# Regrouped score and value matmuls, two row transposes in every auction step, and six float64 weight units converted after the experts

## The chip, the cores and the metric

The kernel runs on one core of a Trainium2 chip. The metric is the device time of one execution in microseconds (us). TensorE multiplies, ScalarE (ACT), VectorE (DVE) and GpSimd (POOL) work beside it, and SyncE's queue (SP) issues nearly all transfers.

## What is computed

Attention with a sigmoid in place of the softmax, then a mixture of experts in which each expert takes exactly 224 tokens by a greedy auction, then a dense layer with a squared ReLU:

```python
attn = 1 / (1 + np.exp(-(q @ k.T / np.sqrt(64) - np.log(448))))   # 4 batches, 12 heads, 448 tokens
x = (attn @ v)                                                    # as 1792 rows of 768
logits = x @ w_gate                                               # 8 experts; greedy, 224 tokens each
h = np.maximum(x[mask] @ w1[e], 0) @ w2[e]                        # w1 768x1024, w2 1024x768
g = s * np.maximum(h @ w_in, 0) ** 2 + b                          # w_in 768x2048, float64
out = g @ w_out                                                   # w_out 2048x768, float64
```

`w_in` and `w_out` arrive as float64. The kernel reads them as pairs of 32-bit words and rebuilds float32 with integer operations.

## The kernel before

**Attention** goes over 24 pairs of heads (`pairs`, six to a batch). For pair n the scores are four chunks of 112 keys. A chunk is two matmuls, one for each head, that stand in different halves of the array's rows (64 rows each) and write one `psc` tile of two banks; ACT turns it into a chunk of `attn` by a sigmoid (L238). The values of pair i are eight matmuls into one bank `pv`, the two heads in different halves of the array's columns; ACT copies it to `xT` (L252 before). `scores_av(n, i)` writes both together: two score chunks of the next pair, two value chunks of this pair, two score chunks, two value chunks. `psc` has two buffers (`ps_s`), `pv` two, and the router's small tiles `plg` and `pt` one each (`ps_l`). `mid` puts the router's matmuls (`gate`, `gate_turn`) between the chunks: a part of them stands inside a pair of score chunks.

**The conversion** of the float64 weights runs on DVE below attention: 32 units of 768 KB come in (`cv_in`, `craw`, three buffers), four DVE instructions make float32 (`convert`, L155 to L158), and 384 KB go out to `narrow` in device memory (`cv_out`). `CONV` says how many units each pair converts. All loads and stores of this part are issued in program order by SP; at most eight of them are under way, since each of the eight DMA semaphores is waited for before it is used again. `load_qk` runs three pairs ahead, `load_v` two.

**The auction** follows: `gate_last` and `prefs` finish the logits, then ten steps (`auction`) each make one small matmul chain through DVE and ACT. While they run, PE turns `xT` back into rows: one turn is four transposes into `px` (three buffers), one ACT copy to `xrow` and one store to `xs`; the first four stores are issued by ACT (`SYNC`), the rest by SP. `ROWS` says how many turns each step makes; one turn stands ahead of the first step. After the last step, `places` builds the index lists, and `gather(0)` fetches the first expert's rows once all of `xs` is written.

**Four groups** of two experts follow. Each group ends with the dense layer for its 448 tokens: a second stage of 16 blocks `f` (18 matmuls each, then ReLU on ACT and three DVE instructions that write `gt`) and a third stage of two halves `h` over 8 weight units, whose sums go to the tile `orow` and are scattered to the output. `advance` keeps the weights ahead: it loads a unit (`raw`, four buffers), rounds it on ACT (`wh`, up to five units ahead of the use) and takes the remainder on DVE or POOL (`wl`, up to four ahead, that is three whole blocks before it is multiplied). Units come in the order of use; the 32 converted units are used in every group.

Of the kernel before, what the change touches and what calls it, by code (L numbers as in the profile page):

```python
# [40 lines left out]
ROWS = (2, 2, 2, 3, 3, 3, 2, 2, 2, 2)  # L41
SYNC = 4
SIGNS = 2
CONV = [1, 1, 2, 1, 2] * 4 + [1, 2, 1]
# [17 lines left out]
def tile_kernel(ctx, tc, qT, kT, v, wg, w1, w2, wi, wo, s2, b2, cst, out):  # L62
# [69 lines left out]
    todo, coming, cout, craw = list(range(len(wide))), [], [], {}  # L132
# [13 lines left out]

    def convert():
        if not coming:
            return
        i = coming.pop(0)  # L150
        r = craw.pop(i)
        lo, hi = r[:, :, 0], r[:, :, 1]
        b = cgp.tile([128, 768], I32, name="cb_", bufs=2)
        a = cgp.tile([128, 768], I32, name="co", bufs=3)
        V.tensor_scalar(a, hi, 3, 0x3FFFFFFF, op0=ALU.logical_shift_left, op1=ALU.bitwise_and)  # L155
        V.tensor_scalar(b, lo.bitcast(U32), 2.0 ** -29, None, op0=ALU.mult)
        V.scalar_tensor_tensor(a, hi, -(1 << 30), a, op0=ALU.bitwise_and, op1=ALU.bitwise_or)
        V.tensor_tensor(a, a, b, op=ALU.add)  # L158
        cout.append((i, a))
        cv_out(1)  # L160
        cv_in()
# [48 lines left out]
    def load_v(i):  # L210
        b, p = pairs[i]
        vt[i] = vp.tile([CP, NC, 128], F32, name="vt", bufs=4)
        nc.sync.dma_start(vt[i], v[b, p])
# [9 lines left out]
    def scores_av(n, i, mid):  # L223
        if n is not None:
            rq, rk = raw_qk.pop(n)
            attn[n] = at.tile([CP, 2, NC, S], F32, name="attn")
        if i is not None:
            a = attn.pop(i)
            pv = ps_v.tile([128, 512], F32, name="pv")
        for c2 in range(0, NC, 2):  # L230
            for c in (c2, c2 + 1):
                mid(c)
                if n is not None:
                    p = ps_s.tile([CP, 2, 512], F32, name="psc")
                    for j in range(2):
                        me = slice(j * D, (j + 1) * D)
                        T.matmul(p[:, j, :S], rk[me, c * CP:(c + 1) * CP], rq[me], start=True, stop=True)  # L237
                    A.activation(attn[n][:, :, c, :], p[:, :, :S], AF.Sigmoid, bias=nls[:CP],  # L238
                                 scale=1.0 / math.sqrt(D))
            for c in (c2, c2 + 1):  # L240
                if i is not None:
                    for j in range(2):
                        T.matmul(pv[j * 64:(j + 1) * 64, :S], vt[i][:, c, j * D:(j + 1) * D], a[:, j, c, :],  # L243
                                 start=(c == 0), stop=(c == NC - 1))
        if i is not None:
            b, p = pairs[i]
            xt = xT[:, p, b * S:(b + 1) * S]
            if i == len(pairs) - 1:
                A.copy(xt[:, :2 * CP], pv[:, :2 * CP])
                A.copy(xt[:, 2 * CP:], pv[:, 2 * CP:S])  # L250
            else:
                A.copy(xt, pv[:, :S])  # L252

    def gate(b, p0, p1, last):
        if p0 == 0:
            plg[b] = ps_l.tile([128, 512], F32, name="plg")
# [9 lines left out]
    def gate_turn(b, stop):  # L266
        lg = lgs.pop(b)
        pt = ps_l.tile([128, 512], F32, name="pt")
# [21 lines left out]
    def bracket(stage):  # L290
# [4 lines left out]
        elif stage == 1:  # L295
            pm = ps_l.tile([128, 512], F32, name="plg")
# [4 lines left out]
        else:  # L301
            pr = ps_l.tile([128, 512], F32, name="plg")
# [31 lines left out]
    cv_in()  # L334
    cv_in()
    cv_in()
    scores_av(0, None, lambda c: None)
# [14 lines left out]
    for i in range(N):  # L352
        b, p = pairs[i]
        if i + 2 < N:
            load_v(i + 2)
        if i + 3 < N:
            load_qk(i + 3)
        def mid(c):
            if b == B - 1 and p == 5:
                if c == 0:  # L360
                    gate(b, 0, 5, 5)
                elif c == 2:
                    gate_copy(b)
                elif c == 3:
                    gate_turn(b, False)
            elif p == 5 and c == 0:
                gate(b, 0, 4, 6)
            elif p == 0 and b and c == 1:
                gate(b - 1, 4, 6, 6)
            elif p == 0 and b and c == 3:  # L370
                gate_copy(b - 1)
            elif p == 1 and b and c == 0:
                gate_turn(b - 1, True)

        scores_av(i + 1 if i + 1 < N else None, i, mid)
        if p == 1 and b:
            prefs(b - 1)
        if b == B - 1 and 2 <= p <= 4:
            bracket(p - 2)
# [5 lines left out]
        if i < N - 1:  # L385
            for _ in range(CONV[i]):
                convert()
    gate_last(B - 1)
# [33 lines left out]
    got = rows_in(1)  # L422
# [288 lines left out]

    stores, out_rows = [], []
# [4 lines left out]
    for g in range(4):  # L717
# [7 lines left out]
        gn = gt[:, :, :, t0:t0 + S]  # L725
        for f in range(KG):
# [7 lines left out]
            V.tensor_scalar(gn[:, f, 0], r, sb2[:, 1:2], None, op0=ALU.add)  # L734
# [4 lines left out]
            advance()  # L739
        gather(2 * g + 3)  # L740
# [96 lines left out]
```

## Time and profile before

| | us |
|---|---|
| median of 3 runs | 968.11 (963.48 to 972.67) |
| the profiled execution | 965.9 |
| its span in the trace | 964.1 |
| PE busy | 937.4 (97% of the span) |
| PEld (weight loads, beside PE) | 782.4 (81%) |
| DVE busy | 563.9 (58%) |
| ACT busy | 443.8 (46%) |
| POOL busy | 137.4 (14%) |

PE's busy time counts each matmul with a modelled end, so 97% is not 97% of its peak. The granted clock of PE is 1.00 (2.4 GHz) in all of attention and nearly all of the groups, and 0.50 (1.2 GHz) in most of the auction. A row of a timeline is the start, the time, the engine, the line, the operation and its tiles, how many were merged, and in square brackets the idle time ahead of it and what ended it.

### The profile page before, as it was taken

The numbers are of one execution on the slowest core, as the hardware profiler recorded it, in microseconds if no ns is written. First come the engines' busy times: TensorE is split into PE (matmuls) and PEld (weight loads), VectorE is DVE, ScalarE is ACT, GpSimd is POOL, SyncE is SP. The second block draws the span as 40 slices with busy tenths as digits, with TensorE's granted clock in tenths as the row PEclk, the third lists the DMA queues.
The fourth block names the chain that finished last, engine by engine and source line by source line (L and its number), as shares of the span: only waits on it lengthen the run. The fifth ranks groups of instructions, "written<-read, shape, count | busy, mean of one in ns | idle before, by whom it ended". The sixth has DMA issues, their size and how long they took to land.

```text
span 964.1 us, 14094 instructions
## 1 busy us (share of the span) xinstructions
PE 937.4 (97%) x5277; PEld 782.4 (81%) x5277; DVE 563.9 (58%) x1015; ACT 443.8 (46%) x771; POOL 137.4 (14%) x136
## 2 busy tenths in 40 slices
PE   9999999778999999999999999999999999999997
PEld 3333333466899999999999999999999999999997
DVE  3565635764777774278677321877774278677320
ACT  5666666573564332266533223664332266433220
POOL 1000001223330000153100002430000152100001
PEclk9999999857999999999999999999999999999999
DMA  8999996272674434477443433774434476533411
GB/s 288 380 318 360 351 374 230 98 228 79 208 232 145 124 114 137 131 244 234 142 138 108 127 99 91 262 233 147 118 116 140 131 235 204 152 121 109 119 46 66
DMA packets 68456, 173.08 MB, mean 180 GB/s; under 512 B 7968, under 2 KB 24864, under 8 KB 68384
## 3 DMA queue, kind: packets, MB, share of 16 engines
q1 hardware_dynamic: 64256, 160.22, 51.5%
q0 software_dynamic: 2272, 11.01, 3.3%
q10 hardware_dynamic: 1856, 0.92, 0.3%
q8 instruction: 42, 0.69, 0.3%
q14 instruction: 30, 0.25, 0.1%
HBM read 148.52 MB, written 23.59 MB: 179 GB/s over the span
## 4 chain that ended last, share of the span: by engine, by line
PE 82%; DVE 6%; DMA 5%; issue 3%; ACT 2%; POOL 1%; SPq 1%; POOLq 0%; ACTq 0%; DVEq 0%
PE acc L642 9%; PE acc L708 8%; PE acc L710 8%; PE acc L709 8%; PE acc L759 8%; PE acc L761 8%; PE acc L760 8%; PE pv L243 7%; PE psc L237 7%; PE acc L643 5%; DVE wl L198 2%; DMA raw<-in_w_dram 2%; DMA rq<-in_qT_dram 2%; PE px L409 2%; ACT wh L187 1%
## 5 line engine op out<-in xcount | busy, mean ns | idle before, releaser
L187 ACT CAST wh<-raw 128x768 fp32r<-128x768 f32 (+1 forms) x240 | 209.2, 878 | 160.1 <-PE acc L761 133.8
L198 DVE TENSOR_TENSOR wl<-raw,wh 128x768 fp32r<-128x768 f32 (+1 forms) x198 | 210.5, 1068 | 104.9 <-ACT wh L187 104.9
L198 POOL TENSOR_TENSOR wl<-raw,wh 128x768 fp32r<-128x768 f32 (+1 forms) x42 | 92.1, 2201 | 433.4 <-ACT wh L187 285.2
L759 PE MATMUL acc<-wh,gt 128*128 128x384 f32 x448 | 149.9, 335 | 0.0
L760 PE MATMUL acc<-wl,gt 128*128 128x384 f32 x448 | 149.7, 334 | 0.0
L761 PE MATMUL acc<-wh,gt 128*128 128x384 f32 x448 | 149.6, 334 | 0.0
L708 PE MATMUL acc<-y,wh 128*128 128x448 f32 x384 | 141.4, 368 | 0.0
L710 PE MATMUL acc<-y,wl 128*128 128x448 f32 x384 | 140.6, 366 | 0.0
L709 PE MATMUL acc<-y,wh 128*128 128x448 f32 x384 | 140.6, 366 | 0.0
L642 PE MATMUL acc<-u,wh 128*128 128x448 f32 x384 | 121.7, 375 | 1.7 <-DVE u L666 1.5
L238 ACT ACTIVATE attn<-psc,nls 112x896 f32<-112x896 f32 x96 | 92.1, 1005 | 53.8 <-PE psc L237 53.8
L732 ACT ACTIVATE r<-acc 128x448 f32<-128x448 f32 x64 | 34.9, 545 | 150.9 <-PE acc L710 150.9
L643 PE MATMUL acc<-u,wl 128*128 128x224 f32 x384 | 101.5, 264 | 0.0
L642 PE MATMUL acc<-x,wh 128*128 128x448 f32 x288 | 95.3, 385 | 0.0
L237 PE MATMUL psc<-rq,rk 64*112 64x448 f32 x384 | 85.6, 561 | 1.1 <-ACT attn L238 0.6
L760 PEld LDWEIGHTS acc<-wl,gt 128*128 128x128 f32 x448 | 84.1, 188 | 0.0
L759 PEld LDWEIGHTS acc<-wh,gt 128*128 128x128 f32 x448 | 84.1, 188 | 0.0
L761 PEld LDWEIGHTS acc<-wh,gt 128*128 128x128 f32 x448 | 84.1, 188 | 0.0
L243 PE MATMUL pv<-attn,vt 112*64 112x448 f32 x384 | 82.8, 552 | 0.0
L643 PE MATMUL acc<-x,wl 128*128 128x224 f32 x288 | 77.2, 268 | 2.1 <-POOL wl L198 2.1
L733 DVE SCALAR_TENSOR_TENSOR r<-r,sb 128x448 f32<-128x448 f32 x64 | 43.8, 685 | 60.4 <-ACT r L732 60.3
L642 PEld LDWEIGHTS acc<-u,wh 128*128 128x128 f32 x384 | 72.0, 188 | 8.6 <-DVE u L666 3.3
(214 smaller groups left out, 1245.3 us busy)
## 6 DMA issues: line engine op xcount, KB each, us to landing
raw<-nw SPq DMA_DIRECT2D x128, 384.0 KB, 3.0
raw<-in_w_dram SPq DMA_DIRECT2D x64, 384.0 KB, 3.7
raw<-in_w_dram SPq DMA_DIRECT2D x48, 512.0 KB, 4.4
craw<-in_wi_dram SPq DMA_DIRECT2D x16, 768.0 KB, 7.6
nw<-co SPq DMA_DIRECT2D x32, 384.0 KB, 8.0
craw<-in_wo_dram SPq DMA_DIRECT2D x16, 768.0 KB, 6.9
rk<-in_kT_dram SPq DMA_DIRECT2D x24, 224.0 KB, 9.2
rq<-in_qT_dram SPq DMA_DIRECT2D x24, 224.0 KB, 8.4
```

The source lines that it names most:

```text
L187: A.copy(h[:, :k], raws[i][:, :k])
L198: eng.tensor_sub(lo[:, :k], r[:, :k], h[:, :k].bitcast(F32))
L237: T.matmul(p[:, j, :S], rk[me, c * CP:(c + 1) * CP], rq[me], start=True, stop=True)
L243: T.matmul(pv[j * 64:(j + 1) * 64, :S], vt[i][:, c, j * D:(j + 1) * D], a[:, j, c, :], start=(c == 0), stop=(c == NC - 1))
L642: T.matmul(p[:, :2 * CAP], wh[:, k], src[:, k].rearrange("p a s -> p (a s)"), start=(k == 0), stop=False)
L643: T.matmul(p[:, :CAP], wl[:, k], src[:, k, 0], start=False, stop=(k == n - 1))
L708: T.matmul(p, wh, src[:, k, 0], start=first, stop=False)
L709: T.matmul(p, wh, src[:, k, 1], start=False, stop=False)
L710: T.matmul(p, wl, src[:, k, 0], start=False, stop=last)
L759: T.matmul(ps[t][:, :DH], hi, wh[:, cols], start=(f == 0), stop=False)
L760: T.matmul(ps[t][:, :DH], hi, wl[:, cols], start=False, stop=False)
L761: T.matmul(ps[t][:, :DH], lo, wh[:, cols], start=False, stop=(f == KG - 1))
```

## The change

1. `scores` and `values` take the place of `scores_av`. Values of pair i come as one run of eight matmuls; behind it come the last two score chunks of pair i+1 and the first two of pair i+2. The router's matmuls stand between these runs. `psc` gets a third buffer; `pv` and one tile `small` for all router work get one bank each. `load_qk` runs four pairs ahead, `load_v` three, with `qk` and `vt` at five buffers.
2. `ROWS` is 2 in all ten steps, three turns stand ahead of the first, and the one that is left is done in `places`.
3. `CONV` covers 26 units. The last 6 (`LATE`) are converted in the first group, one after the blocks f = 1, 4, 7, 10 and 13 of the second stage and one after the first unit of the third stage, in the memory of `orow`, which is single: load, convert, store, next load. In that group `gt`'s first part is written by ACT instead of DVE.

```diff
-ROWS = (2, 2, 2, 3, 3, 3, 2, 2, 2, 2)
+ROWS = (2, 2, 2, 2, 2, 2, 2, 2, 2, 2)
-CONV = [1, 1, 2, 1, 2] * 4 + [1, 2, 1]
+CONV = [1, 1, 1, 1, 2] * 4 + [1, 1, 0]
+LATE = 6
-    qk = att.enter_context(tc.tile_pool(name="qk", bufs=4))
+    qk = att.enter_context(tc.tile_pool(name="qk", bufs=5))
-    ps_s = att.enter_context(tc.tile_pool(name="ps_s", bufs=2, space=PSUM))
-    ps_v = att.enter_context(tc.tile_pool(name="ps_v", bufs=2, space=PSUM))
+    ps_s = att.enter_context(tc.tile_pool(name="ps_s", bufs=3, space=PSUM))
+    ps_v = att.enter_context(tc.tile_pool(name="ps_v", bufs=1, space=PSUM))
...
+    def to_float(a, b, r):
+        lo, hi = r[:, :, 0], r[:, :, 1]
+        V.tensor_scalar(a, hi, 3, 0x3FFFFFFF, op0=ALU.logical_shift_left, op1=ALU.bitwise_and)
+        V.tensor_scalar(b, lo.bitcast(U32), 2.0 ** -29, None, op0=ALU.mult)
+        V.scalar_tensor_tensor(a, hi, -(1 << 30), a, op0=ALU.bitwise_and, op1=ALU.bitwise_or)
+        V.tensor_tensor(a, a, b, op=ALU.add)
...
+    def scores(n, c0, c1):
...
+        for c in range(c0, c1):
+            p = ps_s.tile([CP, 2, 512], F32, name="psc")
+            for j in range(2):
+                me = slice(j * D, (j + 1) * D)
+                T.matmul(p[:, j, :S], rk[me, c * CP:(c + 1) * CP], rq[me], start=True, stop=True)
+            A.activation(attn[n][:, :, c, :], p[:, :, :S], AF.Sigmoid, bias=nls[:CP], scale=1.0 / math.sqrt(D))
+    def values(i):
+        a, v = attn.pop(i), vt.pop(i)
+        pv = ps_v.tile([128, 512], F32, name="pv")
+        for c in range(NC):
+            for j in range(2):
+                T.matmul(pv[j * 64:(j + 1) * 64, :S], v[:, c, j * D:(j + 1) * D], a[:, j, c, :],
+                         start=(c == 0), stop=(c == NC - 1))
...
-    scores_av(0, None, lambda c: None)
+    scores(0, 0, NC)
+    scores(1, 0, 2)
...
-        scores_av(i + 1 if i + 1 < N else None, i, mid)
+        values(i)
+        scores(i + 1, 2, NC)
+        scores(i + 2, 0, 2)
+        if p == 0 and b:
+            gate_turn(b - 1, True)
             prefs(b - 1)
+        elif p == 4:
+            gate(b, 0, 4 if b < B - 1 else 5, 6 if b < B - 1 else 5)
...
+        elif p == 5 and b < B - 1:
+            gate(b, 4, 6, 6)
+            gate_copy(b)
...
+    gate_turn(B - 1, False)
     gate_last(B - 1)
...
-    got = rows_in(1)
+    got = rows_in(3)
...
+    def late_in():
+        i = last["i"]
+        if i < len(wide):
+            src, k, n = wide[i]
+            nc.sync.dma_start(last["buf"][:, :1536], src[n].bitcast(I32).rearrange("p k c -> p (k c)"))
+
+    def late_convert():
+        i = last["i"]
+        buf = last["buf"]
+        to_float(buf[:, 1536:2304], buf[:, 2304:], buf[:, :1536].rearrange("p (c two) -> p c two", two=2))
+        nc.sync.dma_start(narrow[i].rearrange("p k c -> p (k c)"), buf[:, 1536:2304].bitcast(F32))
+        last["i"] += 1
+        late_in()
...
-            V.tensor_scalar(gn[:, f, 0], r, sb2[:, 1:2], None, op0=ALU.add)
+            if g:
+                V.tensor_scalar(gn[:, f, 0], r, sb2[:, 1:2], None, op0=ALU.add)
+            else:
+                A.activation(gn[:, f, 0], r, AF.Identity, bias=sb2[:, 1:2])
...
+            if not g and f % 3 == 1:
+                late_convert()
...
+                if not g and not h and span == [0]:
+                    late_convert()
```

PE's order in the loop over pairs, around the first batch's router (`plg` before). Before, from the values of pair 4's second half on:

```order
L243 MATMUL pv_424<-attn_381,vt_324 64x448 x4
L259 MATMUL plg_476<-xT_86,wgs_85 32x448 x4
L237 MATMUL psc_481<-rq_379,rk_377 112x448 x2
L237 MATMUL psc_485<-rq_379,rk_377 112x448 x2
L243 MATMUL pv_475<-attn_423,vt_375 64x448 x4
L237 MATMUL psc_493<-rq_379,rk_377 112x448 x2
L237 MATMUL psc_497<-rq_379,rk_377 112x448 x2
L243 MATMUL pv_475<-attn_423,vt_375 64x448 x4
L237 MATMUL psc_523<-rq_421,rk_419 112x448 x2
L259 MATMUL plg_476<-xT_86,wgs_85 32x448 x2
L237 MATMUL psc_529<-rq_421,rk_419 112x448 x2
```

Of the change, from pair 4's values on (`small` is the router's tile):

```order
L245 MATMUL pv_429<-attn_363,vt_301 64x448 x8
L235 MATMUL psc_439<-rq_299,rk_297 112x448 x2
L235 MATMUL psc_443<-rq_299,rk_297 112x448 x2
L235 MATMUL psc_448<-rq_341,rk_339 112x448 x2
L235 MATMUL psc_452<-rq_341,rk_339 112x448 x2
L260 MATMUL small_456<-xT_86,wgs_85 32x448 x4
L245 MATMUL pv_485<-attn_405,vt_343 64x448 x8
L235 MATMUL psc_495<-rq_341,rk_339 112x448 x2
L235 MATMUL psc_499<-rq_341,rk_339 112x448 x2
L235 MATMUL psc_504<-rq_383,rk_381 112x448 x2
L235 MATMUL psc_508<-rq_383,rk_381 112x448 x2
L260 MATMUL small_456<-xT_86,wgs_85 32x448 x2
```

A pair had two runs of four value matmuls and two runs of four score matmuls; it now has one run of eight of each, and no router matmul stands inside a run.

DVE's order in the first group's second stage, blocks f = 0 to 1, before (`wl` is the remainder of a weight unit):

```order
L733 SCALAR_TENSOR_TENSOR r_3230<-r_3230,sb2_76 128x448
L734 TENSOR_SCALAR gt_3210<-r_3230,sb2_76 128x448
L735 SCALAR_TENSOR_TENSOR gt_3210<-r_3230,sb2_76,gt_3210 128x448
L198 TENSOR_TENSOR wl_3239<-raw_3090,wh_3183 128x768
L733 SCALAR_TENSOR_TENSOR r_3264<-r_3264,sb2_76 128x448
L734 TENSOR_SCALAR gt_3210<-r_3264,sb2_76 128x448
L735 SCALAR_TENSOR_TENSOR gt_3210<-r_3264,sb2_76,gt_3210 128x448
L198 TENSOR_TENSOR wl_3271<-raw_3121,wh_3241 128x768
L198 TENSOR_TENSOR wl_3273<-raw_3150,wh_3243 128x768
```

And of the change, the same blocks and the start of f = 2:

```order
L750 SCALAR_TENSOR_TENSOR r_3178<-r_3178,sb2_76 128x448
L755 SCALAR_TENSOR_TENSOR gt_3156<-r_3178,sb2_76,gt_3156 128x448
L200 TENSOR_TENSOR wl_3187<-raw_3036,wh_3129 128x768
L750 SCALAR_TENSOR_TENSOR r_3212<-r_3212,sb2_76 128x448
L755 SCALAR_TENSOR_TENSOR gt_3156<-r_3212,sb2_76,gt_3156 128x448
L200 TENSOR_TENSOR wl_3219<-raw_3067,wh_3189 128x768
L200 TENSOR_TENSOR wl_3221<-raw_3096,wh_3191 128x768
L150 TENSOR_SCALAR orow_3157<-orow_3157 128x768
L151 TENSOR_SCALAR orow_3157<-orow_3157 128x768
L152 SCALAR_TENSOR_TENSOR orow_3157<-orow_3157 128x768
L153 ISA orow_3157<-orow_3157 128x1536
L750 SCALAR_TENSOR_TENSOR r_3250<-r_3250,sb2_76 128x448
```

One instruction of each block is gone from DVE (ACT has it), and four stand behind the remainders of every third block. On SP, the store of the converted unit and the load of the next follow there, between loads of weights:

```order
L181 DMA raw_3217<-nw9_147 128x768
L722 DMA nw26_164<-orow_3157 128x768
L716 DMA orow_3157<-in_wo_dram 128x1536
L181 DMA raw_3255<-nw10_148 128x768
L181 DMA raw_3292<-nw11_149 128x768
L181 DMA raw_3322<-nw12_150 128x768
L722 DMA nw27_165<-orow_3157 128x768
```

The store waits for DVE's four instructions, and the weight loads behind it wait with it.

## Rows read from the trace of the kernel before

**Rows 1.** Windows of 20 us: stretch, busy time by engine, granted clock, DMA share, GB/s.

```profile
40.00:60.00 20.00, 20.00 (x104) 6.85 (x102) 9.13 (x14) 11.66 (x14) 0.00 (x0) 1.00 1.03 374
```

**Rows 2.** Chain that ended last, in attention: start, us, engine, tile, line, records.

```profile
45.69 1.65 PE pv L243 x8
47.34 1.69 PE psc L237 x8
...
50.68 0.94 PE psc L237 x4
...
58.44 0.88 PE pt L271 x8
```

**Rows 3.** Timeline, the start of attention.

```profile
5.67 1.90 ACT L238 ACTIVATE attn<-psc,nls 112x896 f32<-112x896 f32 x2 [3.44 <-PE psc L237]
...
9.74 0.28 PEld L237 LDWEIGHTS psc<-rq,rk 64*112 64x112 f32 x4 [0.62 <-ACT attn L238]
...
22.96 1.76 PE L237 MATMUL psc<-rq,rk 64*112 64x448 f32 x8 [0.53 <-DMA rq<-in_qT_dram]
```

**Rows 4.** Timeline, one run of scores and its sigmoid.

```profile
29.66 1.76 PE L237 MATMUL psc<-rq,rk 64*112 64x448 f32 x8
...
30.77 1.90 ACT L238 ACTIVATE attn<-psc,nls 112x896 f32<-112x896 f32 x2 [0.47 <-PE psc L237]
```

**Rows 5.** Timeline, the end of attention.

```profile
173.29 1.69 PE L259 MATMUL plg<-xT,wgs 128*32 128x448 f32 x10 [0.77 <-DVE mm L304]
...
179.62 0.95 PE L276 MATMUL pt<-wgs,xT 128*112 128x8 f32 x8 [0.45 <-ACT xT L249]
```

**Rows 6.** Timeline of ACT in the auction: a copy, its issue, first tests of steps.

```profile
187.03 0.59 ACT L416 COPY xrow<-px 112x512 f32<-112x512 f32 x1 [0.38 <-ACT xrow L416]
187.64 0.31 ACTq L417 DMA_DIRECT2D xs<-xrow  x1
...
197.77 0.39 ACT L456 ACTIVATE junk<-LM,dv 128x112 bf16<-128x112 f32 x1 [0.75 <-DVE LM L452]
...
201.59 0.39 ACT L456 ACTIVATE junk<-LM,dv 128x112 bf16<-128x112 f32 x1 [0.75 <-DVE LM L452]
...
208.38 0.39 ACT L456 ACTIVATE junk<-LM,dv 128x112 bf16<-128x112 f32 x1 [0.60 <-DVE LM L452]
...
211.37 0.39 ACT L456 ACTIVATE junk<-LM,dv 128x112 bf16<-128x112 f32 x1 [0.61 <-DVE LM L452]
```

**Rows 7.** Chain that ended last: the transposes of one auction step of two turns.

```profile
208.08 1.89 PE px L409 x8
```

**Rows 8.** Timeline of `places`: the count's matmul, the index matmuls, the first gather.

```profile
219.75 0.19 PE L486 MATMUL pb<-on,ok 128*1 128x1 f32 x2 [1.45 <-DVE ok L484]
...
219.87 2.64 PE L525 MATMUL pi<-R,oh 112*128 112x16 bf16 x32
...
223.14 1.18 POOL L539 DMA_INDIRECT xr<-xs,idx  x1 [4.65 <-DVE idx L529]
```

**Rows 9.** Transfers by line: the stores of rows issued by SP, median us to landing.

```profile
xs<-xrow SPq DMA_DIRECT2D x20, 224.0 KB, 3.8
```

**Rows 10.** Timeline of DVE, one block of the first group's second stage.

```profile
325.08 0.69 DVE L733 SCALAR_TENSOR_TENSOR r<-r,sb 128x448 f32<-128x448 f32 x1 [0.96 <-ACT r L732]
...
326.89 0.95 DVE L198 TENSOR_TENSOR wl<-raw,wh 128x768 fp32r<-128x768 f32 x1
...
328.79 0.69 DVE L733 SCALAR_TENSOR_TENSOR r<-r,sb 128x448 f32<-128x448 f32 x1 [0.95 <-ACT r L732]
```

**Rows 11.** Timeline of DVE: first instructions of two conversions, back to back.

```profile
13.96 0.56 DVE L155 TENSOR_SCALAR co<-craw 128x768 int32<-128x768 int32 x1 [3.44 <-DMA craw<-in_wi_dram]
...
16.76 0.55 DVE L155 TENSOR_SCALAR co<-craw 128x768 int32<-128x768 int32 x1
```

**Rows 12.** Windows in the first expert: PE waiting for `wl`, and the stretch behind.

```profile
240.00:243.00 3.00, 0.94 (x6) 0.62 (x5) 2.75 (x3) 0.34 (x1) 2.83 (x5) 0.98 0.00 0
243.00:246.00 3.00, 3.00 (x14) 2.81 (x12) 0.29 (x1) 0.00 (x0) 1.97 (x1) 0.50 0.76 255
```

More of the change, by code (lines that the diff above doesn't have):

```diff
@@ L130, in tile_kernel @@
         narrow.append(dpool.tile([128, k, 128], F32, name=f"nw{len(narrow)}"))
-    todo, coming, cout, craw = list(range(len(wide))), [], [], {}
+    todo, coming, cout, craw = list(range(len(wide) - LATE)), [], [], {}
     def cv_in():
@@ L150, in convert @@
         i = coming.pop(0)
-        r = craw.pop(i)
-        lo, hi = r[:, :, 0], r[:, :, 1]
-        b = cgp.tile([128, 768], I32, name="cb_", bufs=2)
         a = cgp.tile([128, 768], I32, name="co", bufs=3)
[L155 to L158, printed above, removed]
+        to_float(a, cgp.tile([128, 768], I32, name="cb_", bufs=1), craw.pop(i))
         cout.append((i, a))
@@ L211, in load_v @@
         b, p = pairs[i]
-        vt[i] = vp.tile([CP, NC, 128], F32, name="vt", bufs=4)
+        vt[i] = vp.tile([CP, NC, 128], F32, name="vt", bufs=5)
         nc.sync.dma_start(vt[i], v[b, p])
@@ L221, in load_qk @@
         raw_qk[i] = (rq, rk)
-    def scores_av(n, i, mid):
-        if n is not None:
-            rq, rk = raw_qk.pop(n)
+    def scores(n, c0, c1):
+        if n >= len(pairs):
+            return
+        if c0 == 0:
             attn[n] = at.tile([CP, 2, NC, S], F32, name="attn")
[L227 to L252, printed above, removed]
@@ new lines, in scores @@
+        rq, rk = raw_qk[n]
+        for c in range(c0, c1):
[4 more added lines that the diff above has]
+            A.activation(attn[n][:, :, c, :], p[:, :, :S], AF.Sigmoid, bias=nls[:CP], scale=1.0 / math.sqrt(D))
+        if c1 == NC:
+            raw_qk.pop(n)
+    def values(i):
[5 more added lines that the diff above has]
+                         start=(c == 0), stop=(c == NC - 1))
+        b, p = pairs[i]
+        xt = xT[:, p, b * S:(b + 1) * S]
+        if i == len(pairs) - 1:
+            A.copy(xt[:, :2 * CP], pv[:, :2 * CP])
+            A.copy(xt[:, 2 * CP:], pv[:, 2 * CP:S])
+        else:
+            A.copy(xt, pv[:, :S])
@@ L254, in gate @@
     def gate(b, p0, p1, last):
         if p0 == 0:
-            plg[b] = ps_l.tile([128, 512], F32, name="plg")
+            plg[b] = ps_l.tile([128, 512], F32, name="small")
         for p in range(p0, p1):
@@ L267, in gate_turn @@
         lg = lgs.pop(b)
-        pt = ps_l.tile([128, 512], F32, name="pt")
+        pt = ps_l.tile([128, 512], F32, name="small")
         pts[b] = pt[:CP, :NC * E].rearrange("p (c e) -> p c e", e=E)
@@ L295, in bracket @@
         elif stage == 1:
-            pm = ps_l.tile([128, 512], F32, name="plg")
+            pm = ps_l.tile([128, 512], F32, name="small")
             T.transpose(pm[:2, :CP], mm[:CP], ident[:CP, :CP])
@@ L301, in bracket @@
         else:
-            pr = ps_l.tile([128, 512], F32, name="plg")
+            pr = ps_l.tile([128, 512], F32, name="small")
             T.matmul(pr[:, :2], on[:2], dg, start=True, stop=True)
@@ L334, in tile_kernel @@
     cv_in()
+    load_qk(3)
+    load_v(2)
     cv_in()
     cv_in()
-    scores_av(0, None, lambda c: None)
+    scores(0, 0, NC)
+    scores(1, 0, 2)
     nc.sync.dma_start(sb2[:, 0:1], s2.partition_broadcast(128))
@@ L710, in full_mm @@
         T.matmul(p, wl, src[:, k, 0], start=False, stop=last)
+    last = {"i": len(wide) - LATE}
+    def late_in():
[10 more added lines that the diff above has]
+        late_in()
     stores, out_rows = [], []
@@ L725, in tile_kernel @@
         gn = gt[:, :, :, t0:t0 + S]
+        if not g:
+            last["buf"] = ml.tile([128, 3072], I32, name="orow")
+            late_in()
         for f in range(KG):
@@ L745, in tile_kernel @@
             tiles = [(c - 64, ids) for c, ids in tiles]
-        orow = ml.tile([128, 4, DM], F32, name="orow")
         for h in range(2):
@@ L762, in tile_kernel @@
                     if span[-1] == n - 1:
+                        if not h and not t:
+                            orow = ml.tile([128, 4, DM], F32, name="orow")
                         dst = orow[:, t, h * DH:(h + 1) * DH]
```

30 lines of the change are left out of this document (8 added, 22 removed).

## Prediction

> **What bounds the kernel now.** The table of engines says PE, with 97% of the span, but that is an average over stages, so I went by windows and the chain of waits. In attention PE is the bound without a gap: in 20 us it is busy for 20.00, with ACT at 11.66 and DVE at 9.13 [rows 1]. In the same window the DMA engines are at 1.03, 374 GB/s [rows 1]; they are the next limit, and nobody waits for them yet but once (0.53 us for a query tile) [rows 3]. In the auction PE, DVE and ACT pass one small result round, and the chain of waits shows the row transposes on the path [rows 7]. In the groups PE is the bound again, fed by weights that are prepared ahead. So a saving counts if it is PE time in attention or a link of the auction's loop; DVE time in the groups counts only if weights come late.
>
> **The switch, which is the main term.** The reader is to compare two rows of the chain: a run of four score matmuls (8 records) takes 1.69 us, and one that is cut in two by the router takes 0.94 for each half [rows 2]. Twice 0.94 is 1.88, so to start a run costs 1.88 - 1.69 = 0.19, and four records of streaming 0.75. A run of four value matmuls takes 1.65 [rows 2]; with the same streaming its start costs 1.65 - 1.50 = 0.15. The two kinds use the array differently (halves of rows, halves of columns), and I take the 0.19 and 0.15 as the price of changing from one to the other.
>
> The change has 24 value runs where 48 stood: 24 x 0.15 = 3.6. Score runs inside the loop go from 45 to 23: 22 x 0.19 = 4.2. Three cuts by the router's second part are gone: 3 x 0.19 = 0.6. Together -8.4 us. From below, this term is nothing, if the start costs are paid per four matmuls whatever stands ahead; no run of eight stands in the trace.
>
> The Trainium skill, "TensorE: Matmul & The Clock Gate", section "Step-by-step: what each phase is for", puts the drain of the array at about 128 cycles. At 2.4 GHz that is an estimate of 0.05 us a switch; over the 49 starts and cuts it would give 2.6 us in place of 8.4. The rows show three times as much at each start, and I keep the rows.
>
> **The rest of attention.** With a third `psc` buffer the start is shorter. The sixth chunk's weights load at 9.74, released by ACT [rows 3]. ACT starts at 5.67 and does two chunks in 1.90 [rows 3], so about 0.9 from start to start and 1.0 each; run without gaps it ends the third chunk at 5.67 + 1.8 + 1.0 = 8.5, and with three buffers that is the release: -1.2 (from below 0, if the second pair's keys land later). The wait of 0.53 goes, since loads run a pair deeper: -0.5 [rows 3]. PE's 0.77 for the threshold chain [rows 5], which stood behind two conversions on DVE, goes too, as the chain now starts a pair earlier and one conversion stands ahead: -0.8. At the end, the last `gate_turn` (0.88 [rows 2]) leaves the middle of the value run and comes behind it, over the 0.45 in which PE waits for ACT's copy [rows 5]: 0.88 saved, 0.5 paid, -0.4. Attention in sum: -8.4 - 1.2 - 0.5 - 0.8 - 0.4 = -11.3 us.
>
> Six units less make 6 x 1.18 = 7.1 MB less to move here (768 KB in and 384 KB out each). The 49 MB that are left (72 tiles of 224 KB, 26 units, the constants, four weight units) need 131 us at 374 GB/s [rows 1], and PE still works for over 150. That cover holds.
>
> **The auction.** A step with three turns takes 201.59 - 197.77 = 3.82 us, one with two 211.37 - 208.38 = 2.99 [rows 6]. Three steps change: -2.5. Two more turns stand ahead of the first step. Their transposes lie under DVE's work on the last logits, but their copies (0.59) and issues (0.31) [rows 6] are on ACT ahead of its first tests: 1.8 us, of which the same copies leave the second step and some lie under the wait for DVE. I charge 0.6, between 0 and 1.8. The auction: -1.9.
>
> **`places`.** The left-over turn stands on PE between the count's matmul and the index matmuls, which take 2.64 us [rows 8]. Four transposes are half of 1.89 [rows 7], and the index matmuls start that much later: +1.0. The first gather [rows 8] also waits for this turn's store, which takes 3.8 from issue to landing [rows 9]: transposes done at 219.94 + 0.95 = 220.9, copied at 221.5, landed at 225.3, against an index list ready at 223.14 + 1.0 = 224.1. So +1.0 to +2.2. I take 1.1, since the store meets idle queues.
>
> **The first group.** DVE's block is 2.76 us from the start of `r` to the end of `wl` (326.89 + 0.95 - 325.08), in a period of 3.71 [rows 10]. ACT's pass for `gt` costs DVE about 0.1 more of waiting than its own instruction cost; no row shows an ACT pass of this form, so I keep 0 to 0.5. A conversion takes 16.76 - 13.96 = 2.80 [rows 11], one in three blocks: 0.93 a block. DVE then needs 2.76 + 0.1 + 0.93 = 3.8 of 3.71. It falls behind by 0.1 to 0.5 a block, 1 to 6 us by f = 13. The cover is the lead of the remainders, three blocks or 11 us, so I charge 0.2. Loads queued on SP behind the store that waits for DVE (three between two conversions) wait for a remainder of the next block anyway; they lose nothing until that lead is used up. The six conversions leave attention at no gain of their own, as DVE was hidden there.
>
> **The sum.** -11.3 - 1.9 + 1.1 + 0.2 = -11.9 us. The profiled execution took 965.9, so 954.0. The median of the three runs, 968.1, lies 2.2 above that execution; put on top, 956.2, and I say 956.
>
> **Rivals.**
> *The runs' start is no switch.* Then the 8.4 us stay, and only 3.5 are won: 964.6; if a third of the starts' price is a switch, 961.8. For it: no run of eight is in the trace. Against it: the halves of 0.94 show that a start has a price of its own, and a change of kind is all that the starts have in common. Chance 0.13, a result of 962 to 965. (By the drain of "TensorE: Matmul & The Clock Gate" in the Trainium skill, as an estimate, it would be 962.)
>
> *Sigmoid cannot follow a run of eight.* The fourth chunk of a run needs the first one's buffer. PE comes to it 0.1 + 3 x 0.75 = 2.35 us after the run's start; ACT starts 1.11 after it and takes 1.0, which frees the buffer at 2.1 [rows 4]. That is a slack of 0.2. If ACT comes late by more, each run goes at ACT's pace, four times 0.95 against 0.19 + 3.0: 0.6 x 22 = 13 us, and 969. The Trainium skill, "TensorEngine Tiling (Array Packing)", section "PSUM Bottleneck", warns of just this, that emptying PSUM may become the bottleneck once matmuls run in parts of the array. Against it: over a whole pair ACT needs 4 x 0.95 and a copy, under 4.5 us of 6.3. Chance 0.08; half of these cases keep part of the gain.
>
> *Late weights in the first group (slower than before).* If DVE falls behind by more than 11 us, or a conversion waits long for its 768 KB, PE stops for `wl`. In the first expert such a stop left PE 0.94 busy in 3 us, and the clock fell from 0.98 to 0.50 (the level of 1.2 GHz) for the 3 us behind [rows 12]. Six conversions that each cost 2.80 and half of those 3 us make 26 us: 956 + 26 = 982. It decides only from about 0.8 us a block of overload on. Chance 0.06.
>
> The remaining 0.73 is the forecast. Its own range is 951 to 962: the start may give 0 instead of 1.2, the auction 1.2 less, `places` 1.1 more, the first group up to 2 more, and runs of one kernel lie some us apart.
>
> **Chances.** A measurement of this kernel can tell about 1%, or 9.7 us, from no change; that bound is 958.4. Of the forecast's 0.73 about 0.66 lie below it; of the rivals, 0.02 (part of the gain kept). Faster 0.68. Within 1%: the rest of the forecast, the first rival, most of the second, 0.27. Slower 0.05, from the third. The range is 949 to 964: it takes in the forecast and the first rival but for its last half us, and leaves out the second and third.
>
> **What would show it.** In the trace of the changed kernel a score run of 16 records should take 3.2 us and a value run 3.15, a pair 6.3 instead of 6.7, and the first index work should start near 168 instead of 179.6 [rows 5]. Runs of 3.8 with PE waiting for the sigmoid would show the second rival, runs of 3.4 and 3.3 the first. Every auction step should take 2.99, the first two a little more; the first gather should start some 12 us earlier than 223.14 [rows 8]. In the second stage of the first group, PE's blocks should keep 3.71; a wait of PE for `wl` would show the third rival.

## The result, and the profile after

| | us | ratio to before, 95% interval |
|---|---|---|
| before, beside it | 966.97 (4 runs, 963.48 to 972.67) | |
| changed kernel | 954.50 (4 runs, 954.23 to 956.53) | 0.9873 (0.9840 to 0.9905) |
| changed kernel, measured again (e9) | 953.84 (5 runs, 952.96 to 955.80) | 0.9884 (0.9857 to 0.9911) |

It is 12 us faster, and 1.5 us under the forecast of 956. The profiled execution took 954.64 with a span of 952.9, against a sum of 954.0 on that basis. Where the 11.2 us of span were won can be followed by the start of the same work in both traces:

| start of | before | after | won so far |
|---|---|---|---|
| first score matmul | 4.61 | 5.20 | -0.59 |
| first value matmul | 10.68 | 10.30 | 0.38 |
| index matmuls behind attention | 179.62 | 168.91 | 10.71 |
| first gather | 223.14 | 211.76 | 11.38 |
| first expert matmul | 230.64 | 219.54 | 11.10 |
| first Relu of the first group's second stage | 302.07 | 291.22 | 10.85 |
| end of the span | 964.1 | 952.9 | 11.2 |

The first score matmul comes later because the zero matmuls that stand ahead of it take longer; the timeline of before has

```profile
1.19 3.49 PE L320 MATMUL psc<-zero 128*112 128x512 bf16 x9 [1.19 <-DVE zero L316]
```

and that of the changed kernel

```profile
1.18 4.09 PE L321 MATMUL psc<-zero 128*112 128x512 bf16 x9 [1.18 <-DVE zero L317]
```

Nearly all of the gain is attention (10.71 of 11.2); auction and `places` together give 0.7, and everything behind the gather moves it by less than 0.6. The window of attention that answers to [rows 1] (stretch, busy time by engine, granted clock, DMA share, GB/s) shows PE full as before, with less DMA under it:

```profile
40.00:60.00 20.00, 20.00 (x110) 7.75 (x108) 7.78 (x15) 12.52 (x15) 0.00 (x0) 1.00 0.79 281
```

The chain of waits in attention (start, us, engine, tile, line, records) is to be held against [rows 2]. There is one run of each kind to a pair, of 3.16 and 3.19 us, back to back:

```profile
50.25 3.16 PE pv L245 x16
53.41 3.19 PE psc L235 x16
56.60 0.88 PE small L272 x8
57.48 3.16 PE pv L245 x16
```

The timeline of PE shows the end of attention, where the index matmuls [rows 5] have no wait in brackets any more. From 10 us to the end of attention the table of PE's waits is empty; before, it named 0.8 us for the threshold chain, 0.5 for a query tile and 0.4 for ACT's copy:

```profile
168.10 0.95 PE L272 MATMUL small<-ct,lg 128*112 128x8 f32 x8
168.91 0.93 PE L277 MATMUL small<-wgs,xT 128*112 128x8 f32 x8
```

In the auction the chain (three steps, seen at the instruction of DVE that ends each) has a period of 2.98 to 2.99, where the kernel before had 3.80 to 3.82 in three steps (one of them in [rows 6]):

```profile
182.13 0.17 DVE jd L472 x2
...
185.11 0.18 DVE jd L472 x2
...
188.10 0.17 DVE jd L472 x2
```

In `places`, the chain shows the left-over turn between the count's matmul and the gather. The timelines of PE and DVE show the index matmuls, which took 2.64 us before [rows 8], and the index list, and in a fence by itself the index list of before; that of POOL shows what the gather waited for. The index list was ready at 210.0 and the store had landed at 210.84; the gather left at 211.76:

```profile
206.70 0.19 PE pb L484 x2
206.89 1.05 PE px L407 x4
207.96 0.59 ACT xrow L414
208.57 2.27 DMA xs<-xrow
```

```profile
207.71 1.90 PE L523 MATMUL pi<-R,oh 112*128 112x16 bf16 x32
209.77 0.24 DVE L527 SCALAR_TENSOR_TENSOR idx<-pi,ia 128x8 int32<-128x8 f32 x2 [0.64 <-ACT ia L526]
```

```profile
222.66 0.24 DVE L529 SCALAR_TENSOR_TENSOR idx<-pi,ia 128x8 int32<-128x8 f32 x2 [0.49 <-ACT ia L528]
```

```profile
211.76 1.18 POOL L537 DMA_INDIRECT xr<-xs,idx  x1 [6.32 <-DMA xs<-xrow]
```

In the first group's second stage the timeline of DVE shows one block from `r` to the next `r`, 304.89 - 302.01 = 2.88 us with a wait for ACT in it. The timeline of ACT shows the first and the last Relu, and the window shows that PE stood still nowhere:

```profile
302.01 0.68 DVE L750 SCALAR_TENSOR_TENSOR r<-r,sb 128x448 f32<-128x448 f32 x1
303.43 0.69 DVE L755 SCALAR_TENSOR_TENSOR gt<-r,sb,gt 128x448 fp32r<-128x448 f32 x1 [0.74 <-ACT gt L754]
304.03 0.95 DVE L200 TENSOR_TENSOR wl<-raw,wh 128x768 fp32r<-128x768 f32 x1
304.89 0.68 DVE L750 SCALAR_TENSOR_TENSOR r<-r,sb 128x448 f32<-128x448 f32 x1
```

```profile
291.22 0.55 ACT L749 ACTIVATE r<-acc 128x448 f32<-128x448 f32 x1 [2.42 <-PE acc L708]
...
351.21 0.53 ACT L749 ACTIVATE r<-acc 128x448 f32<-128x448 f32 x1
```

```profile
280.00:350.00 70.00, 70.00 (x367) 65.22 (x366) 53.49 (x80) 33.37 (x60) 2.66 (x2) 1.00 0.62 199
```

### The profile page after: what moved, and what is told of

Read it like the earlier page. It is cut to its first block, busy times and chain, and to the rows that moved or that the text cites. A ratio compares the mean times of both kernels' runs of the same rounds, so it can differ in the third digit from the quotient of the medians.

```text
span 952.9 us, 14071 instructions
## 1 busy us (share of the span) xinstructions
PE 926.7 (97%) x5277; PEld 784.7 (82%) x5277; DVE 554.8 (58%) x999; ACT 450.9 (47%) x787; POOL 137.7 (14%) x136
## 4 chain that ended last, share of the span: by engine, by line
PE 84%; DVE 5%; DMA 5%; issue 2%; ACT 2%; POOL 1%; POOLq 0%; ACTq 0%; SPq 0%; DVEq 0%
PE acc L640 9%; PE acc L706 8%; PE acc L707 8%; PE acc L708 8%; PE psc L235 8%; PE acc L780 8%; PE acc L782 8%; PE acc L781 8%; PE pv L245 8%; PE acc L641 4%; DMA raw<-in_w_dram 4%; DVE wl L200 3%; PE px L407 2%; ACT wh L189 1%; DMA xr<-xs,idx 1%
## 5 line engine op out<-in xcount | busy, mean ns | idle before, releaser
L236 ACT ACTIVATE attn<-psc,nls 112x896 f32<-112x896 f32 x96 | 89.0, 1009 | 13.7 <-PE psc L235 13.7
L235 PE MATMUL psc<-rq,rk 64*112 64x448 f32 x384 | 78.8, 549 | 0.0
L245 PE MATMUL pv<-attn,vt 112*64 112x448 f32 x384 | 77.5, 545 | 0.0
L708 PEld LDWEIGHTS acc<-y,wl 128*128 128x128 f32 x384 | 72.1, 188 | 5.9
```

The costliest lines, as they stand in the source:

```text
L245: T.matmul(pv[j * 64:(j + 1) * 64, :S], v[:, c, j * D:(j + 1) * D], a[:, j, c, :], start=(c == 0), stop=(c == NC - 1))
L708: T.matmul(p, wl, src[:, k, 0], start=False, stop=last)
```

## The experiments

Diffs are against the changed kernel.

**Two runs a pair (e1).** Is the gain the number of switches, or did the third buffer and the deeper loads bring it?

```diff
...
-        values(i)
+        values(i, 0, 2)
         scores(i + 1, 2, NC)
+        values(i, 2, NC)
         scores(i + 2, 0, 2)
```

> The values of a pair are again made in two halves, with the scores of the next pairs between them (v 0-1, s, v 2-3, s); the third psc buffer, the deeper loads, the late units and the new auction all stay. Theory (each change between value and score matmuls costs TensorE 0.15 to 0.19 us): runs of 8 records of 1.65 (values) and 1.69 (scores) us, a pair 6.68 instead of 6.35, attention from the first value matmul to the last 7.8 us longer than in the changed kernel (24 x 0.15 + 22 x 0.19), the time near 962.3. Rival (the gain came with the third buffer and the deeper loads, or the start's price is paid per four matmuls whatever stands ahead): a pair stays at 6.35, the time at 954.5.

Measured: 962.49 us (10 runs), ratio 0.9963 (0.9944 to 0.9982); that is 0.0090, or 8.7 us, above the changed kernel's ratio. In its trace the index matmuls start at 177.0, 8.1 later; 0.5 of this lies ahead of the first value matmul (10.82 against 10.30), so from there on it is 7.6. The chain of waits shows the runs of before, though buffers and loads are the new ones:

```profile
104.81 1.69 PE psc L235 x8
106.50 1.65 PE pv L249 x8
108.16 1.69 PE psc L235 x8
```

So the runs themselves are worth some 8 us, and the rival falls.

**Four runs a pair (e2).** Is it a fixed price for each change of kind?

```diff
...
-        values(i)
-        scores(i + 1, 2, NC)
-        scores(i + 2, 0, 2)
+        for c in range(NC):
+            values(i, c, c + 1)
+            n, k = divmod(c + 2, NC)
+            scores(i + 1 + n, k, k + 1)
```

> One chunk of values, one chunk of scores, in turn: four runs of each kind in a pair where the changed kernel has one. Theory (a fixed price for each change of kind): three more changes to either kind in a pair, 3 x (0.15 + 0.19) = 1.0 us a pair, runs of 4 records of 0.90 and 0.94, about 23 us more in attention than the changed kernel, three times the loss of two runs a pair; the time near 978. Rival (the price is not one of the change of kind, but of something that stands twice in a pair): no more than the 7.8 us of two runs a pair, or nothing.

Measured: 992.95 us (one run), index matmuls at 203.1, 34.2 later than in the changed kernel, not 23. Chain of waits:

```profile
52.24 0.94 PE psc L235 x4
53.18 0.90 PE pv L249 x4
54.08 0.94 PE psc L235 x4
```

The rows are those expected: 3.19, 1.69 and 0.94 for 16, 8 and 4 score records lie on a line of 0.75 for four records and 0.19 for the start; 3.16, 1.65 and 0.90 on one of 0.755 and 0.14 to 0.15. What was not expected stands in the table of PE's waits for attention (line, releaser: us in all, times, longest):

```profile
PE pv L249 <- ACT xT L260: 8.0, 13, 0.7
```

`ps_v` has one buffer. A short score run no longer covers ACT's copy of the pair before, so the first value run waits for it. Without these 8.0, 26.2 are left where 23 were expected; what makes up the other 3 is open.

**Two psc buffers (e3).** Could ACT's sigmoid have stopped the long runs?

```diff
-    ps_s = att.enter_context(tc.tile_pool(name="ps_s", bufs=3, space=PSUM))
+    ps_s = att.enter_context(tc.tile_pool(name="ps_s", bufs=2, space=PSUM))
```

> The score chunks go through two psc buffers instead of three, all else as in the changed kernel. Theory (a run of four score chunks must wait for the sigmoid of the chunk two ahead of it): the third chunk of a run can't start before ScalarE has done the first, about 0.1 + 0.8 + 1.1 + 1.0 after the run's start against 1.6 without a wait; a run then goes at ScalarE's pace and takes about 3.9 us instead of 3.19, 0.7 x 22 = 15 us more, the time near 969. Rival (two buffers do, and the third bought nothing but the start): 954.5 to 955.5, no wait of TensorE for ScalarE in the runs.

Measured: 972.66 us (one run), index matmuls at 187.0, 18.1 later. One score run in the chain of waits, now cut in two by ACT:

```profile
51.36 0.96 PE psc L235 x4
...
52.34 1.02 ACT attn L236
...
53.40 1.91 PE psc L235 x8
```

From 51.36 to 55.31 it takes 3.95 in place of 3.19: 0.76 x 22 = 16.7, and the first value matmul comes at 11.68 in place of 10.30. This is the wait that the second rival of the prediction named, at 0.76 us a run where it gave 0.6; the third buffer is what keeps it away.

**The old order of the auction's turns (e4, timed as e10).**

```diff
-ROWS = (2, 2, 2, 2, 2, 2, 2, 2, 2, 2)
+ROWS = (2, 2, 2, 3, 3, 3, 2, 2, 2, 2)
...
-    got = rows_in(3)
+    got = rows_in(1)
```

> The auction's turns stand as in the kernel before (one row ahead of the first step, three in the fourth to sixth, none left for the index part), all else as in the changed kernel. Theory: the fourth to sixth steps take 3.82 again instead of 2.99 and the first two lose what the extra row cost them, so the auction is 2.3 us longer; the index part is 1.7 us shorter, as its matmuls come right behind the count and the gather no longer waits for a late store; the first gather some 0.7 us later than in the changed kernel, the time 955. Rival (the turns of the first step cost as much as they save): gather 1 to 2 us earlier than in the changed kernel, and the new order of rows is a loss.

> The same kernel as e4 (the auction's turns as in the kernel before, the rest as in the changed one), now timed, since one execution of it showed the clock come back to 1.00 in two of its three steps of three turns. Theory (e4's execution is typical): those steps take 2.94 in this trace too, the first gather comes 1 to 2 us earlier than in the changed kernel, the time is 1 to 2 us under the changed kernel's on this chip, and the even turns were a loss here. Rival (the clock stays at 0.50, as in the kernel before): three steps of 3.82, the gather 0.7 us later than in the changed kernel, the time 0.7 us above it.

Measured: e4 953.24 (one run); e10 954.99 (5 runs), ratio 0.9883 (0.9857 to 0.9910), beside 0.9884 for the changed kernel on the same chip. In the time the two can't be told apart, with intervals of 2.6 us to either side; the way there differs. The timeline of PE in e4 shows the three steps of three turns. The first takes 2.81 for its transposes, the others 1.52:

```profile
182.27 2.81 PE L407 MATMUL px<-ident,xT 128*112 128x128 f32 x12
...
186.03 1.52 PE L407 MATMUL px<-ident,xT 128*112 128x128 f32 x12
```

The windows of the same trace say why: the granted clock rises from 0.50 to 1.00 (1.2 to 2.4 GHz) behind the first of them.

```profile
182.00:185.00 3.00, 3.00 (x16) 2.77 (x16) 1.54 (x13) 2.30 (x9) 0.54 (x2) 0.50 0.78 192
185.00:188.00 3.00, 1.99 (x19) 1.59 (x18) 2.09 (x18) 2.10 (x9) 0.81 (x2) 0.93 0.87 266
188.00:191.00 3.00, 2.02 (x18) 1.58 (x17) 2.08 (x18) 2.83 (x10) 0.80 (x2) 1.00 1.02 321
```

With the faster clock ACT's tests end the step, after 2.94. In e10 the rise came behind the second such step, and in the trace of before it did not come at all: 3.80 to 3.82 three times (one of them in [rows 6]). Why the same table of turns gave three courses of the clock was not settled. With two turns in every step there was one course: in the ten traces with that table (the changed kernel twice, e1 to e3, e5 to e8 and e11) the clock, once fallen to 0.50 early in the auction, stays there until the gather has left. Counted from the index matmuls behind attention, the first gather leaves 41.6 us later in e4, 42.3 in e10, 42.9 in the changed kernel (twice, e9 as well) and 43.5 before. So here the old order has the gather up to 1.3 us earlier, and the even turns with a left-over one are a small loss at that point. That win is given back in the first expert. There PE's waits in e10 (219 to 291 us) and its windows behind the gather are these:

```profile
PE acc L641 <- POOL wl L200: 3.2, 1, 3.2
```

```profile
213.00:225.00 12.00, 9.56 (x51) 8.06 (x50) 3.30 (x8) 4.86 (x11) 2.73 (x4) 0.83 0.42 116
225.00:237.00 12.00, 8.77 (x44) 8.06 (x44) 4.18 (x9) 4.33 (x11) 7.86 (x18) 0.74 0.32 108
```

and in the changed kernel:

```profile
PE acc L641 <- POOL wl L200: 0.9, 1, 0.9
```

```profile
213.00:225.00 12.00, 8.66 (x36) 7.08 (x35) 2.33 (x5) 3.32 (x7) 2.80 (x3) 0.68 0.40 116
225.00:237.00 12.00, 11.05 (x79) 10.43 (x79) 5.92 (x12) 6.20 (x16) 8.26 (x18) 1.00 0.36 129
```

In e10 PE is at the full clock sooner, comes sooner to weights that POOL has not prepared, stands for 3.2 us, and goes on with a mean clock of 0.74. From the first expert matmul to the first Relu of the second stage it needs 73.6 us (e4 73.0, with a wait of 3.0), the changed kernel 71.7 (e9 71.5, with a wait of 1.4).

**None late (e5).** All 32 units are converted in attention again.

```diff
-CONV = [1, 1, 1, 1, 2] * 4 + [1, 1, 0]
-LATE = 6
+CONV = [1, 1, 2, 1, 2] * 4 + [1, 2, 1]
+LATE = 0
...
```

> All 32 units are converted in attention, by the table of the kernel before, and the first group's second stage converts none; runs, buffers and auction as in the changed kernel. Theory (DMA still covers): 7.1 MB more in attention, 56 MB in all, 150 us at 374 GB/s, against some 157 of TensorE's work there; the pairs stay near 6.35 us, the time within 2 us of 954.5, and the late conversions bought little. Rival (with the runs shortened, DMA or VectorE becomes the bound of attention): TensorE waits for tiles of q, k or v, up to 8 us in sum, the time 957 to 963, and the late conversions are what lets the regrouping count.

Measured: 957.36 us (4 runs), ratio 0.9904 (0.9878 to 0.9929), so 2 to 3 us above the two measurements of the changed kernel, with intervals that overlap. In attention nothing is lost: in its window PE is busy for 40.00 of 40, with DMA at 0.96, and the index matmuls start at 168.6.

```profile
20.00:60.00 40.00, 40.00 (x212) 15.32 (x208) 20.89 (x33) 25.49 (x31) 0.00 (x0) 1.00 0.96 346
```

The loss comes right behind. The timeline of DVE has the last conversion in front of the copy of the logits, on which the auction waits:

```profile
168.66 0.55 DVE L150 TENSOR_SCALAR co<-craw 128x768 int32<-128x768 int32 x1
...
169.60 2.56 DVE L152 SCALAR_TENSOR_TENSOR co<-craw,co 128x768 int32<-128x768 int32 x1
172.20 0.96 DVE L153 CUSTOM_DVE_ANT_0 co<-co,cb__1372 128x1536 uint16<-128x1536 uint16 x1
173.08 0.18 DVE L281 COPY L<-small 112x32 f32<-112x32 f32 x1
```

In the changed kernel that copy starts at 169.88, 3.2 us earlier. Neither theory had this place. Counted from the index matmuls, the first gather leaves at 45.7 us (changed kernel 42.9) and the first Relu of the second stage is 126.3 behind (122.3); the traced execution is the slowest of the four (960.75). In the kernel before, attention was 11 us longer, and its last conversion ended at 178.6, ahead of the copy at 180.6; the shorter attention has no room for 32 in this order of work. Three instructions of e5's last four conversions take 2.56 to 2.61 us in place of 0.95, each beside a `wl` pass of POOL (passes at 160.25, 166.11 and 169.34). These 4.9 us are more than the 3.2; whether 32 units would fit with POOL's passes elsewhere, no run shows.

**The late conversions twice (e6).**

```diff
+        for _ in range(2):
+            to_float(buf[:, 1536:2304], buf[:, 2304:], buf[:, :1536].rearrange("p (c two) -> p c two", two=2))
-        to_float(buf[:, 1536:2304], buf[:, 2304:], buf[:, :1536].rearrange("p (c two) -> p c two", two=2))
```

> Each of the six late conversions is done twice on VectorE, with the same result. Theory (the lead of the remainders covers VectorE's lag): a block with its share of conversion costs VectorE some 2.9 + 0.1 + 1.87 = 4.8 to 4.9 us in a period of 3.71, so it falls behind by 1.15 a block and some 15 us by f = 13, over the lead of 11; TensorE waits for weights near the end of the first group, 4 to 5 us in sum and a clock that falls behind the wait; the time 959 to 962. Rival (any lag is passed on at once): six times 2.8 = 17 us more; rival (the lead is larger than 15 us): no wait, 954.5.

Measured: 968.32 us (one run), 13.8 above the changed kernel, not 4 to 5. PE's waits between 290 and 380 us, and a window behind the first of them:

```profile
PE acc L708 <- DVE wl L200: 6.7, 3, 3.2
PE acc L782 <- DVE wl L200: 4.1, 1, 4.1
```

```profile
330.00:340.00 10.00, 6.83 (x29) 5.84 (x28) 8.42 (x13) 3.66 (x6) 0.00 (x0) 0.83 0.49 178
```

The lead is as large as was said: five double conversions put 5 x 5.73 = 28.7 us on DVE, 14 blocks of 2.89 in a period of 3.71 take 11.5 off, 17.2 are left, of which PE waited 6.7; so at least 10.5 us were covered, against 11 (the sum leaves out three other passes of some 0.5 us and a second remainder in block f = 1). But the waits of the sixth conversion (4.1) had been left out, and PE's lower clock behind the waits; 10.8 of the 13.8 us are waits, and the granted clock is 0.50 from 336.6 to 340.0 and from 367.3 to 370.7, which makes up about the rest.

**The left-over turn earlier (e7).**

```diff
+        rest()
         for c in range(NCH):
             V.tensor_scalar(oh[:, c], slot[:CP], pos[:, c:c + 1], None, op0=ALU.is_equal)
...
-                rest()
```

> The turn that the auction left over is moved from behind the count's matmul to ahead of the one-hot loop, where TensorE waits 1.46 us for VectorE; all else as in the changed kernel. Theory (the transposes lay on the path and their store's landing was what the gather waited for): transposes in TensorE's idle time, the store some 1.5 us earlier, the index matmuls right behind the count; the first gather 1.5 us earlier than in the changed kernel, the time 953. Rival (the transposes hold up the count's matmul instead, or the copy on ScalarE holds up something there): gather at the same place, 954.5.

Measured: 952.27 us (4 runs), ratio 0.9851 (0.9825 to 0.9876). In the timeline of POOL the gather now waits for the index list, and leaves 0.2 us behind it:

```profile
209.82 1.18 POOL L537 DMA_INDIRECT xr<-xs,idx  x1 [4.65 <-DVE idx L527]
```

Counted from the index matmuls behind attention the gather leaves at 41.2 us (changed kernel 42.9), and the first Relu of the second stage is 120.2 behind (122.3). Nearly all of this is the store; the index list itself is only 0.2 earlier. The transposes had hardly held it up: from the first matmul of `places` to the list's end it is 5.61 us in the kernel before, 5.76 in the changed one and 5.61 in e7. Unlike that of e4 and e10, this win is kept in the first expert: POOL starts its first remainders at 58.6 us (changed kernel 60.7), and PE does not wait for them.

**gt on VectorE (e8).**

```diff
-            if g:
-                V.tensor_scalar(gn[:, f, 0], r, sb2[:, 1:2], None, op0=ALU.add)
-            else:
-                A.activation(gn[:, f, 0], r, AF.Identity, bias=sb2[:, 1:2])
+            V.tensor_scalar(gn[:, f, 0], r, sb2[:, 1:2], None, op0=ALU.add)
```

> In the first group the first part of gt is made on VectorE again, as in the other groups, and not on ScalarE; all else as in the changed kernel. Theory: VectorE waits 0.74 us for that pass of ScalarE in each block, and its own instruction takes 0.45; so on VectorE the block gets shorter by some 0.3, the lag of 3.8 us at the last block falls to about 0, no wait of TensorE either way, the time 954.5. Rival (the change bought VectorE time): VectorE falls further behind, up to 3 us more at the last block.

Measured: 954.55 us (one run). The timeline of DVE has a block of 318.67 - 316.00 = 2.67 us, and ACT's last Relu comes without lag, at 347.65, 56.21 behind the first at 291.44:

```profile
316.00 0.68 DVE L750 SCALAR_TENSOR_TENSOR r<-r,sb 128x448 f32<-128x448 f32 x1
316.71 0.45 DVE L751 TENSOR_SCALAR gt<-r,sb 128x448 fp32r<-128x448 f32 x1
...
318.67 0.68 DVE L750 SCALAR_TENSOR_TENSOR r<-r,sb 128x448 f32<-128x448 f32 x1
```

The move of this pass to ACT costs DVE 0.22 us a block instead of saving it 0.45. It shows in no time, because the lead covers it.

**Both edits (e11), and the changed kernel beside them (e9).**

> The changed kernel as it is, beside the next two on one chip, for a ratio to the kernel before that theirs can be held against, and for a second look at its auction. Expected: 954 to 956, a ratio near 0.988, every auction step but the first two at 2.98 to 2.99 with the granted clock at 0.50.

> The changed kernel with the two edits of e7 and e8 together: the left-over turn ahead of the one-hot loop, and the first part of gt on VectorE in the first group too. Theory: 2 us under the changed kernel on this chip, a ratio near 0.986, all of it from the turn (the store lands early and the index matmuls stand right behind the count); the gt edit shows in VectorE's lag at the last block of the first group (0 instead of 3.8 us) and not in the time. Rival (the gain of e7 was a matter of the run): no difference to the changed kernel.

Measured on one chip: e9 953.84, e11 952.32 (4 runs), ratio 0.9862 (0.9832 to 0.9893). The traces repeat e7: the gather at 41.2 us and the first Relu at 120.4 behind the index matmuls, against 42.9 and 122.6 in e9. In the time it is 1.5 us, and the intervals overlap; the gain is shown in two traces of each kind, and in the time only likely.

## Why the prediction was right, point by point

- **The switch (-8.4).** Right in its mechanism and size. Undoing the runs alone costs 7.6 us from the first value matmul to the index matmuls and 8.7 in the time, where 7.8 were worked out for it (the three cuts by the router, 0.6, stay gone in e1). Three lengths of run lie on one line. The Trainium skill, "TensorEngine Tiling (Array Packing)", section "Key Properties", says that a change of tiling mode drains TensorE. The rows agree that it costs, and put 0.14 to 0.19 us on it. The first rival, that the start of a run is no switch, is out. What in a start takes the time is not shown: in the timeline a run's first weights also load only as it starts (53.34 us for both in the changed kernel), and no run separates this from the drain.
- **The start (-1.2).** 0.38 by the two traces, but the mechanism is right, and the size too where the clock allows it. From the first score to the first value matmul before took 6.07 us; with the third buffer it is 4.85 to 4.89 in the five traces that have the full clock by the first score matmul (e4, e5, e7, e8, e9), so 1.2 is won. The other 0.8 went to the granted clock, which the sum did not have. The zero matmuls (3.49 and 4.09 us) show it: one by one they start 0.43 us apart, and in the kernel before 0.22 apart from 4.1 us on; in the changed kernel they keep 0.43 to the last. The trace's record of the full clock (2.4 GHz) starts at 3.9 us before and at 5.7 after, and between 4.5 and 6.8 in the other traces of the changed kernel and its variants; the later it starts, the later the first value matmul comes (e3 with its two buffers aside). Whether the change has a part in this or the one trace of before was lucky stays open.
- **The waits and the last turn (-1.7).** From the first value matmul to the index matmuls 10.33 were won; less 7.6 for the runs and 0.6 for the cuts that is 2.1. The waits themselves, 0.8, 0.5 and 0.4 in PE's table, are all gone.
- **The auction (-1.9).** 2.34 from the index matmuls behind attention to the first tests of the last step (214.35 before, 201.30 after), so right in size against the trace of before, and the steps are the 2.99 foretold. The 0.6 charged for the two turns ahead was 0.1 (the first tests come 0.4 later, the second step is 0.3 shorter). But the three steps of 3.8 on which the term rests were one course of the clock. With the same table of turns it rose in two other traces, and against those, up to the first matmuls of `places`, the even turns won only 0.4 and 1.1. That the trace of before had the slow course is luck for this term.
- **`places` (+1.1, up to 2.2).** 1.67 from the first matmul of `places` to the gather (5.85 before, 7.52 after), inside the bounds, but not by the terms that made them. The 1.0 for the transposes was wrong: the index matmuls start 0.9 later but take 1.90 in place of 2.64, and the index list is 0.15 later. DVE's one-hot loop, whose results these matmuls read, is over 4.89 us behind that first matmul in both kernels, so it seems to set their end. The store was fast (2.27 us against 3.8 in [rows 9]) and still landed 0.84 behind the list; and the gather left 0.92 behind the landing, where it left 0.24 behind the list before. For that no term stood in the sum. So the wait for the store was named rightly, and that its total came near 1.1 is partly luck. The two terms together were to bring 0.8 and brought 0.7 at the gather; against e10 they bring nothing that the time can show.
- **The first group (+0.2).** DVE was 3.8 us behind at the last block (351.21 against 291.22 + 56.21 = 347.43, the 56.21 being PE's pace for the same Relus before), inside the 1 to 6 foretold; PE did not wait, and e6 found a lead of at least 10.5 us where 11 were assumed, on which the third rival's point of decision rests. The 0.1 for ACT's pass was 0.22 (e8).
- **The step that failed.** "The six conversions leave attention at no gain of their own, as DVE was hidden there." DVE is hidden under PE up to the last pair only. The trace of e5 shows that 32 conversions in the shorter attention put the copy of the logits 3.2 us later. The sum did not suffer, because its end-of-attention terms assumed DVE to be free there, which is what the late units buy. So the regrouping and the late units belong together: without the second the gather comes 2.9 us later behind the index matmuls. In the time it is 2 to 3 of the 12 us, with intervals that overlap.

## What to carry to other kernels

Read the price of a change of matmul kind from two lengths of run in the trace; if the rows lie on a line, fewer and longer runs are worth the number of starts saved, as long as the buffers behind them let the longest run pass. When a stage gets shorter, ask what of the other engines' hidden work no longer ends inside it: that work, not the stage's own bound, stood first on the path behind it. And what a small stage wins can be lost at the next restart, where PE comes earlier to weights that nobody has prepared (e4, e10); it is kept where their preparation moves forward with it (e7).

## What was not expected of the hardware

- The granted clock in the auction took three courses under one table of turns: 0.50 throughout (before), 1.00 after one step of three turns (e4), 1.00 after two (e10). With two turns in every step it stayed at 0.50 in all ten traces.
- A conversion instruction of DVE that takes 0.95 us takes 2.46 to 2.57 when POOL's `wl` runs beside it (in the changed kernel at 154.30 and 161.01, with POOL's passes at 154.00 and 160.53). The Trainium skill, "SBUF — State Buffer", section "SBUF: two separate sides", says that VectorE and GpSimd share a pair of ports as an exclusive lock, which an instruction of VectorE with two inputs in SBUF needs, so that the later one blocks. The trace agrees: at 161.01 the instruction ends at 163.58, 0.82 behind POOL's pass (162.76). Three such instructions stand in e5's last four conversions.
- Handing a 0.45 us pass from DVE to ACT made DVE's block longer by 0.22 us, since DVE then waits 0.74 us for the result (e8).
